# Attention and a highway layer on one core: batch 0 by query tiles, k and v in other layouts, and part of x turned by DMA

## The chip, the cores and the metric

One core of a Trainium2 chip. The metric is device time in microseconds (us), the median of the runs shown. Beside it stands one profiled execution, whose trace all views are taken from. Five engines each work through their own list: PE (TensorE: matrix products), ACT (ScalarE: functions of one operand), DVE (VectorE), POOL (GpSimd) and SP (which only issues DMAs). ACT and POOL issue DMAs too.

## What is computed

Eight batches, twelve heads, 448 positions, 64 dimensions per head. Cosine attention, and then a highway layer on rows of 768 (shortened):

```python
q_n = q / (norm(q) + 1e-6);  k_n = k / (norm(k) + 1e-6)
scores = q_n @ k_n.T / tau
attn = softmax(scores)
x = (attn @ v).transpose(0, 2, 1, 3).reshape(B * S, H * D)     # 3584 x 768
H = relu(x @ w_h);  T = sigmoid(x @ w_t + b_t)
out = T * H + (1 - T) * x
```

## The kernel before

**Layout.** The 448 queries of a head are split as l * 7 + j (64 values of l, 7 of j). q of a batch lies with the even heads on 64 partitions and the odd ones on the other 64, one l to a partition, so that a row of one head is 7 x 64 contiguous numbers (448 numbers, 1,792 bytes). Heads are worked on in six pairs (head p and p + 6), and the pairs in three groups g of two. x of a batch is [128, 7, 384]: FFN tile i of 0 to 2 is the 128 queries of two values of j, with its two halves of the heads in x[:, 2i : 2i + 2]; tile 3, the "tail", is the 64 queries of j = 6, with the two halves of the heads on the two halves of the partitions.

**Per batch,** in the names that the program gives to its operations:

- loads: q in fp32 on SP's queue (`ldq`, L297, L299); k and v cast to fp16 on POOL's queue (`ldk` L309, `ldv` L327 and L331) for the first 384 positions, three to a partition; the last 64 positions of k and v in fp32 on SP's queue (`ldkt` L314, `ldvt` L320). Batch 0 takes k in fp32 into the output buffers `os` instead (`ldf` L305). The gate's and the layer's weights come once, cast, on POOL's queue (L335);
- norms: squares on ACT (L368 q, L388 and L391 k, L402 k's tail), sums over 64 numbers on DVE (L376, L397, L404), then the inverse root by two Newton steps in seven short DVE instructions (L416 to L423, `nt`);
- scaling: POOL multiplies q (L434), k (L495) and k's tail (L502), DVE some of the first; PE turns them (`tq` L446: 7 products with the identity, `tk8` L460 and L465: 8), DVE copies them out of PSUM (L451, L471, L473, L475);
- scores of a pair: three groups `qk` of two products side by side (L531: 64 rows, 128 columns of weights, 448 moving columns) and one `qkt` for the tail (L542); ACT takes the exp of each 128 x 448 (L537, L544), seven per pair;
- values: for each pair three groups `av` (one product L556 and six L561, weights are 128 queries of the exps) and one `avt` for the last 64 queries (L569, 8 products); column 65 of v is 1, so the sum of the exps comes along; DVE takes its reciprocal and writes x (L576, L577, `rc` and `ev`);
- FFN, for each of the four tiles: PE turns x (`xt6` L600, six products with the identity, three in the tail), DVE copies to xT (L602, `cpx`); the gate's and the layer's products (`ff`, halves of three products each: L616, tail L613); DVE adds the bias (L625, `za`), ACT takes tanh (L632), DVE the rest (L634, L628, L637), POOL adds x into `os` (L642, for the last two tiles DVE), SP stores (L649 tail, L652).

**What sets the order.** Nothing is scheduled on the chip. A list ORDER (L18 to L95) gives the order of all 1,915 operations, written out as numbers; SLOTS (L97 to L130) gives each buffer. Every engine works its own part of that list from front to back and waits by semaphores for its operands. `PORT` names operations of DVE and POOL between which the order adds a dependence (L133, L723 to L734). Rings of buffers are small: three E (exps of a pair), three x, three xT, four os, eight PSUM banks B.

Where the text below counts operations, they are counted in ORDER, each number resolved to the operation that the program makes under it.

Of the kernel before, what the change touches and what calls it, by code (L numbers as in the profile page):

```python
# [8 lines left out]
FP32 = mybir.dt.float32  # L9
# [84 lines left out]
""".split()  # L94
)  # L95

SLOTS = {  # L97
    "qr": "01010101",
    "kr": "0120120",
    "kt": "01010101",  # L100
    "kb": "01010101",
    "kp": "012345012345012345012345012345021435021435120534",
    "vr": "01010101",
    "vt": "01011010",
    "vp": "01010101",
    "sq": "0120120102102102102102012012022102102102102021020",
# [95 lines left out]
def kernel(  # L202
# [26 lines left out]
    NN = 84  # L229
# [540 lines left out]
```

## Time and profile before

| | |
|---|---|
| median of 3 runs | 270.19 us (269.24 to 270.47) |
| profiled execution | 270.06 us, of it 268.3 us span |
| PE, DVE, ACT, POOL busy | 251.6, 233.4, 214.5, 169.8 us |
| DMA | 51,092 packets, 38.64 MB; queue of SP 25,888 packets, of POOL 24,896 |
| exps L537 and L544 | 288 and 48 instructions, means 577 and 597 ns (they overlap by some 0.1 us) |
| turns of x L600, copies L602 | 168 and 32 instructions |
| landing of wt, wh, the two weights | 20.3 and 24.3 us after issue |

Busy time counts an engine's instructions from start to end; products of PE overlap, so their mean duration (326 ns for 384 columns) is longer than their distance. Idle time of an engine that others don't wait for costs nothing.

### The profile page before, as it was taken

To read this page: it belongs to the slowest core of one execution; us is meant where nothing else is said; L and a number is where in the kernel's file an instruction comes from. 1 tells how busy PE (TensorE), PEld (TensorE's weight loads), DVE (VectorE), ACT (ScalarE), POOL (GpSimd) and SP (SyncE) were. 2 spreads that over 40 slices of the span, in tenths; PEclk is the share of its full clock that TensorE was granted. 3 is DMA by queue.
4 is the path that set the end of the run, shared out by engine and by line. 5 is a ranking of instruction groups with operands and counts; after the bars stand their busy time and mean duration, and the time that the engine had idled before them with its cause. 6 is when DMAs were issued, how large, how long until landed. Compare 5 with 4: busy or idle time off the path is not lost.

```text
span 268.3 us, 7687 instructions
## 1 busy us (share of the span) xinstructions
PE 251.6 (94%) x3042; PEld 158.8 (59%) x3042; DVE 233.4 (87%) x523; ACT 214.5 (80%) x421; POOL 169.8 (63%) x212
## 2 busy tenths in 40 slices
PE   8375999999999999999999999999999999999990
PEld 2122566656756576657656685666666675667660
DVE  2987988799999999999989899999998788657993
ACT  3389899999589997999899996999979757883120
POOL 6467878306975679668957397659555686320650
PEclk9755799999999999999999999999999999999998
DMA  7999999999307990496995972990513101052146
GB/s 173 298 290 181 208 270 261 213 255 126 44 18 221 234 182 14 146 257 159 151 142 185 164 107 67 330 135 4 147 23 100 29 15 49 0 147 65 29 135 190
DMA packets 51092, 38.64 MB, mean 144 GB/s; under 512 B 37488, under 2 KB 47856, under 8 KB 51056
## 3 DMA queue, kind: packets, MB, share of 16 engines
q1 hardware_dynamic: 25888, 26.75, 36.2%
q0 software_dynamic: 24896, 11.21, 33.1%
q8 instruction: 24, 0.39, 0.5%
q10 hardware_dynamic: 272, 0.20, 0.2%
q14 instruction: 12, 0.10, 0.1%
HBM read 38.34 MB, written 11.01 MB: 184 GB/s over the span
## 4 chain that ended last, share of the span: by engine, by line
PE 81%; DMA 6%; DVE 4%; ACT 4%; SPq 1%; issue 1%; POOL 1%; ACTq 0%; DVEq 0%
PE B L616 33%; PE B L531 12%; PE B L561 10%; PE B L613 5%; DMA os<-in_k_dram 4%; PE B L556 4%; PE B L600 4%; PE B L446 3%; PE B L542 3%; PE B L569 3%; PE B L460 3%; ACT E L537 3%; DMA out_dram<-os 1%; PE B L465 1%; DVE hm L628 1%
## 5 line engine op out<-in xcount | busy, mean ns | idle before, releaser
L537 ACT ACTIVATE E<-B 128x448 f16<-128x448 f32 x288 | 137.4, 577 | 15.6 <-PE B L531 12.6
L642 POOL TENSOR_TENSOR os<-x,hm 128x384 f32<-128x384 f16 x53 | 47.5, 911 | 50.2 <-DVE hm L637 39.6
L616 PEld LDWEIGHTS <-xT 128*128 128x128 f16 x576 | 51.2, 98 | 34.8 <-issue 7.5
L434 POOL TENSOR_TENSOR qn<-qr,y 128x448 f16<-128x448 f32 x47 | 43.4, 934 | 24.6 <-issue 8.1
L616 PE MATMUL B<-wh,xT 128*128 128x384 f16 x288 | 57.6, 326 | 0.0
L616 PE MATMUL B<-wt,xT 128*128 128x384 f16 x288 | 56.7, 326 | 0.0
L531 PE MATMUL B<-qT,kT 64*128 64x448 f16 x288 | 43.5, 367 | 2.8 <-DVE kT L473 1.5
L561 PE MATMUL B<-vp,E 128*128 128x65 f16 x864 | 44.5, 195 | 0.0
L561 PEld LDWEIGHTS <-E 128*128 128x128 f16 x864 | 39.1, 99 | 2.9
L632 ACT ACTIVATE tt<-z 128x768 f16<-128x768 f32 (+1 forms) x32 | 25.3, 793 | 18.5 <-DVE z L625 14.8
L495 POOL TENSOR_TENSOR kp<-kr,y 128x384 f16<-128x384 f16 x42 | 34.3, 827 | 8.2 <-DVE tt L634 2.6
L628 DVE SCALAR_TENSOR_TENSOR hm<-B,x 128x384 f16<-128x384 f32 x56 | 30.5, 549 | 3.0 <-PE B L616 1.7
L556 PE MATMUL B<-vp,Et 128*128 128x130 f16 x144 | 32.3, 224 | 0.0
L625 DVE TENSOR_TENSOR z<-B,bias 128x384 f32<-128x384 f32 x48 | 25.9, 551 | 6.5 <-PE B L616 5.5
L544 ACT ACTIVATE Et<-B 128x448 f16<-128x448 f32 x48 | 27.9, 597 | 3.1 <-PE B L542 2.8
L577 DVE SCALAR_TENSOR_TENSOR x<-B,rd 128x448 f16<-128x448 f32 x48 | 29.2, 617 | 0.6
L376 DVE TENSOR_REDUCE n<-sq 128x14 f32<-128x896 f32 (+1 forms) x25 | 25.8, 1040 | 1.2 <-ACT sq L368 1.2
L397 DVE TENSOR_REDUCE n<-sq 128x18 f32<-128x1152 f32 (+2 forms) x17 | 21.5, 1269 | 4.2 <-ACT sq L388 3.8
L368 ACT ACTIVATE sq<-qr 128x896 f32<-128x896 f32 (+1 forms) x24 | 23.1, 978 | 1.1 <-DMA qr<-in_q_dram 1.1
L531 PEld LDWEIGHTS <-kT 64*128 64x128 f16 x288 | 10.3, 94 | 20.1 <-issue 12.3
L556 PEld LDWEIGHTS <-Et 128*128 128x128 f16 x144 | 14.1, 98 | 7.9 <-issue 4.7
L542 PE MATMUL B<-qT,kT 128*128 128x448 f16 x48 | 17.4, 371 | 1.1 <-DVE kT L475 1.1
(59 smaller groups left out, 363.3 us busy)
## 6 DMA issues: line engine op xcount, KB each, us to landing
qr<-in_q_dram SPq DMA_DIRECT2D x7, 1344.0 KB, 7.6
out_dram<-os SPq DMA_DIRECT2D x48, 192.0 KB, 3.3
kr<-in_k_dram POOLq DMA_DIRECT2D x7, 576.0 KB, 12.2
vr<-in_v_dram POOLq DMA_DIRECT2D x7, 576.0 KB, 10.3
kt<-in_k_dram SPq DMA_DIRECT2D x16, 96.0 KB, 6.4
vt<-in_v_dram SPq DMA_DIRECT2D x16, 96.0 KB, 7.5
out_dram<-os SPq DMA_DIRECT2D x16, 96.0 KB, 2.9
qr<-in_q_dram SPq DMA_DIRECT2D x3, 448.0 KB, 6.9
```

What stands on the lines that cost most here:

```text
L434: ENG[eng].tensor_mul(R("qn", 3 * b + g)[:, :, t, :], R("qr", b)[:, g + 3 * t, :].rearrange("l (j d) -> l j d", d=D), R("y", b)[:, c : c + ...
L495: ENG[eng].tensor_mul(R("kp", 6 * b + p).rearrange("l c t d -> l t c d"), a, kcol(b, p))
L531: nc.tensor.matmul(R("B", ("S", n, c, t))[:, 0:S], lhsT=R("kT", i)[ln, s, 128 * c : 128 * c + 128], rhs=R("qT", i)[ln, s, :], start=True, ...
L537: nc.scalar.activation(R("E", n)[:, at : at + 7, :].rearrange("l j x -> l (j x)"), R("B", ("S", n, c, t))[:, 0:S], AF.Exp)
L544: op("ACT", f"expt {n}", lambda: nc.scalar.activation(R("Et", n).rearrange("l j x -> l (j x)"), R("B", ("St", n))[:, 0:S], AF.Exp), r=[("B ...
L556: nc.tensor.matmul(U[:, 2 * c : 2 * c + 2, :], lhsT=Et[:, 2 * c : 2 * c + 2, :].rearrange("l j x -> l (j x)"), rhs=vp[:, 6:8, 0:65], start ...
L561: nc.tensor.matmul(U[:, 2 * c + t, :], lhsT=E[:, at : at + 2, :].rearrange("l j x -> l (j x)"), rhs=vp[:, 3 * t + m, 0:65], start=False, s ...
L577: op("DVE", f"ev {n}", lambda: nc.vector.scalar_tensor_tensor(out=R("x", b)[:, :, D * p : D * p + D], in0=U_()[:, :, 0:D], scalar=0.0, in1 ...
L616: nc.tensor.matmul(P[:, 0:MH], lhsT=xT[:, cc, :], rhs=w_[:, cc, MH * mh : MH * mh + MH], start=(cc == 0), stop=(cc == CC - 1))
L625: op("DVE", f"za {g} {mh}", lambda at=at, sl=sl: nc.vector.tensor_add(R("z", g)[:, sl], R("B", at)[:, 0:MH], biast[:, :] if tail else bias ...
L628: op("DVE", f"hm {g} {mh}", lambda at=at, sl=sl, mh=mh: nc.vector.scalar_tensor_tensor(out=R("hm", g)[:, sl], in0=R("B", at)[:, 0:MH], sca ...
L642: op(eng, f"out {g} {mh}", lambda sl=sl, mh=mh: ENG[eng].tensor_add(R("os", g)[:, sl], xpart(mh), R("hm", g)[:, sl]), r=[("gg", g), ("x", ...
```

## The change

1. **k by 7 positions like q.** `ldk` loads rows of 448 numbers; squares, sums, scaling and turning of k are those of q, without a separate tail. The scaled k lies in [128, 8, 2, 64] with one zeroed piece at either end, and eight turns per group put the middle six positions into three full blocks and the outer ones into the tail's block.
2. **v in four loads on POOL's queue** per batch (two halves of the heads, two of the partitions, 3 or 4 positions each), tails among them; `vt` copies the tail from there.
3. **Batch 0.** Its k comes in fp32 in three parts, the first on ACT's queue, into E buffers. Its inverse roots are exp(-0.5 ln(n + 1e-14)) on ACT (`lnexp`), for which ACT loads table 6 at the start and table 0 behind the third; tanh waits for that. Its attention runs by query tiles: `attend0(g, i)` for tile i of 128 queries (the fourth has 64) and group g, with exps of 512 and 384 columns, and x has a token of its own for each tile, so that FFN tile i reads only its own queries. The turned q and k of its first group lie in an x buffer.
4. **x of batches 1 to 6** is turned into xT by a transposing DMA on SP's queue (`xd`), without PE and DVE; batches 0 and 7 keep `xt` and `cpx`.
5. Rings: xT 5 (was 3), qT and kT 4 (3), no kt, vt, kb; v's zeroes and ones are set by DVE, not POOL. The loads of q of batches 1 on get a dependence on the ACT instruction ahead of them in the order.
6. ORDER and SLOTS are new throughout (1,875 operations).

In the new order `ldf 0` (ACT) and `ldq 0 0` (SP) come first, POOL starts with `ldk 1`, then v of batch 0 and the gate's weights. The first FFN product belongs to tile 0 of batch 0 and stands behind 25 exps of batch 0 in ACT's list; before, it stood behind 52 exps. All counts of exps by width in the new list: 21 of 512 and 21 of 384 for batch 0, 42 of 448 for each later batch, as before.

The core of the diff:

```diff
-    WARM = 18
+    WARM, NF = 18, 0
+    XDMA = range(1, B - 1)
...
+    LG = ((0, 0), (0, 28), (0, 56))
...
-        xT=(3, [128, CC, 128], FP16), z=(2, [128, DM], FP32), tt=(2, [128, DM], FP16), hm=(3, [128, DM], FP16),
+        xT=(5, [128, CC, 128], FP16), z=(2, [128, DM], FP32), tt=(2, [128, DM], FP16), hm=(3, [128, DM], FP16),
...
+    def ld_kf(g, eng):
+        op(eng, f"ldf {g}", lambda: ENG[eng].dma_start(kf(g), q_src(k, 0)[:, :, g::3, :]), w=[("E", ("f", g))])
...
+    def ld_v(b):
+        for t, jj, j0, n in ((0, 0, 0, 4), (0, 1, 4, 3), (1, 0, 0, 3), (1, 1, 3, 4)):
+            def fn(t=t, jj=jj, j0=j0, n=n):
+                c = 64 if (t, jj) == (0, 1) else 0
+                nc.gpsimd.dma_start(R("vr", b)[64 * jj : 64 * jj + 64, 6 * t : 6 * t + 6, c : c + 64 * n].rearrange("l h (c d) -> l h c d", c=n),
+                                    v_src(b)[:, 6 * t : 6 * t + 6, j0 : j0 + n, :])
+            op("POOL", f"ldv{n} {b} {t} {jj}", fn, w=[("vr", b, t, jj)])
...
+    def lnexp(b, lo, hi, parts):
+        i = (b, lo)
+        op("ACT", f"ln{hi - lo} {b} {lo}", lambda: nc.scalar.activation(
+            R("tu", i)[:, 0, lo:hi], R("n2", b)[:, lo:hi], AF.Ln, bias=eps[:, 0:1]),
...
+        op("ACT", f"ie{hi - lo} {b} {lo}", lambda: nc.scalar.activation(
+            R("y", b)[:, lo:hi], R("tu", i)[:, 0, lo:hi], AF.Exp, scale=-0.5),
...
+    def attend0(g, i):
...
+                        for t in range(2):
+                            ln, at = slice(64 * t, 64 * t + 64), unit(s)[0][t][c] - o - 512 * t
+                            nc.tensor.matmul(R("B", (A, B_)[t])[:, at : at + w], lhsT=k_()[ln, s, 128 * c : 128 * c + 128],
+                                             rhs=q_()[ln, s, 128 * i : 128 * i + w], start=True, stop=True)
...
+            for t, X, m in ((0, A, 512), (1, B_, 384)):
+                op("ACT", f"ex{m} {n}", lambda X=X, m=m, t=t, o=o: nc.scalar.activation(
+                    flat()[:, o + 512 * t : o + 512 * t + m], R("B", X)[:, 0:m], AF.Exp),
...
+        def turn_dma():
+            X = R("x", b)
+            nc.sync.dma_start(R("xT", g)[:, 0:nb, :], X[:, 6, :] if tail else X[:, 2 * i : 2 * i + 2, :].rearrange("l j m -> l (j m)"),
+                              transpose=True)
+        if b in XDMA:
+            op("SP", f"xd{nb} {g}", turn_dma, r=[xk], w=[("xT", g)])
+        else:
+            op("PE", f"xt{nb} {g}", turn_x, r=[xk, ("id",)], w=[("B", ("Tx", g))], mode="F")
...
+    op("ACT", "table2", lambda: table(0), r=[("lg", i) for i in LG], w=[("t0",)])
...
         if b == 0:
...
+            for i in range(4):
+                for g in range(NG):
+                    attend0(g, i)
```

More of the change, by code (lines that the diff above doesn't have):

```diff
@@ L144, in __init__ @@
         kind = name.split()[0].rstrip("0123456789")
-        self.port = eng in ("DVE", "POOL") and (kind in PORT or kind == "sqq")
+        self.held = eng == "SP" and kind == "ldq" and name.split()[1] != "0"
+        self.port = eng in ("DVE", "POOL") and (kind in PORT or kind == "sq")
 class Plan:
@@ L220 @@
     NC, NJ = 3, 7
-    WARM = 18
+    WARM, NF = 18, 0
+    XDMA = range(1, B - 1)
+    GROUPS = ((0, 1), (1, 2), (2, 3)), ((0, 1), (1, 3)), ((0, 3),)
+    LG = ((0, 0), (0, 28), (0, 56))
+    SCALE = {("q", 0, 0): ("DVE", "POOL"), ("k", 0, 0): ("DVE", "POOL")}
     tau = float(tau)
@@ L247 @@
     biast = sb.tile([128, MH], FP32, name="biast")
[L248 removed]
+    eps = sb.tile([128, 1], FP32, name="eps")
     wz = sb.tile([128, 640], FP16, name="wz")
@@ L258, in R16, with turned, tn @@
         return R("B", i).bitcast(FP16)
+    def turned(nm, i):
+        if i:
+            return R(nm + "T", i)
+        X = R("x", "f").rearrange("l j m -> l (j m)")
+        return (X[:, 0:896] if nm == "q" else X[:, 896:1920]).rearrange("l (s x) -> l s x", s=2)
+    def tn(nm, i):
+        return (nm + "T", i) if i else ("x", "f", nm)
     ENG = dict(SP=nc.sync, ACT=nc.scalar, POOL=nc.gpsimd, DVE=nc.vector, PE=nc.tensor)
@@ L267, in zero, with table @@
         return fn
-    op("ACT", "table", lambda: nc.scalar.activation(tab[:1, :], nc.const_aps.tensor(0.0, [1, 1]), AF.Exp), w=[("tab",)])
+    def table(n):
+        return nc.scalar.add_instruction(mybir.InstLoadActFuncSet(
+            name=nc.get_next_instruction_name(), engine=nc.scalar.engine, act_func_set_id=n))
+    op("ACT", "table", lambda: table(6), w=[("t6",)])
     op("POOL", "ident", lambda: make_identity(nc, ident), w=[("id",)])
     for i, t in enumerate(TILES["vp"]):
-        op("POOL", f"zvp {i}", zero("POOL", [(t[:, :, 0:6, D : D + 1], 1.0), (t[:, :, 6:8, 0 : D + 1], 0.0),
+        op("DVE", f"zvp {i}", zero("DVE", [(t[:, :, 0:6, D : D + 1], 1.0), (t[:, :, 6:8, 0 : D + 1], 0.0),
                                     (t[0:64, :, 6, D : D + 1], 1.0), (t[64:128, :, 7, D : D + 1], 1.0)]), w=[("zvp",)])
-    for i, t in enumerate(TILES["kb"]):
-        op("DVE", f"zkb {i}", zero("DVE", [(t[0:64, :, 1, :], 0.0), (t[64:128, :, 0, :], 0.0)]), w=[("zkb",)])
-    op("DVE", "zw", zero("DVE", [(wz[:, :], 0.0)]), w=[("wz",)])
+    for i, t in enumerate(TILES["kn"]):
+        op("DVE", f"zkn {i}", zero("DVE", [(t[:, 0, 1, :], 0.0), (t[:, 7, 0, :], 0.0)]), w=[("zkn",)])
+    op("DVE", "zw", zero("DVE", [(wz[:, :], 0.0), (eps[:, :], 1e-14)]), w=[("wz",), ("eps",)])
     for i in range(WARM):
@@ L280, with q_src, v_src, ld_qk @@
                                                          start=True, stop=True), r=[("wz",)], w=[("B", ("W", i)), ("wm",)], mode="F")
-    def q_src(b):
-        return q[b].rearrange("(u s) (l j) d -> s l u (j d)", s=2, j=NJ)
-    def m_src(t, b):
-        return t[b, :, 0 : NC * 128, :].rearrange("h (l c) d -> l h (c d)", c=NC)
-    def t_src(t, b, ab):
-        return t[b, 6 * ab : 6 * ab + 6, NC * 128 : S, :].rearrange("h l d -> l h d")
-    def ld_q(b, gs=range(3), eng="SP"):
+    for i in range(NF):
+        op("PE", f"wf {i}", lambda i=i: nc.tensor.matmul(R("B", ("F", i))[:, :], lhsT=wz[:, 0:128], rhs=wz[:, 128:640],
+                                                         start=True, stop=True), r=[("wz",)], w=[("B", ("F", i))], mode="F")
+    def q_src(t, b):
+        return t[b].rearrange("(u s) (l j) d -> s l u (j d)", s=2, j=NJ)
+    def v_src(b):
+        return v[b].rearrange("h (l j) d -> l h j d", j=NJ)
+    def ld_qk(nm, b, gs=range(3)):
+        t, eng = (q, "SP") if nm == "q" else (k, "POOL")
         def fn():
-            d, a = R("qr", b), q_src(b)
+            d, a = R(nm + "r", b), q_src(t, b)
             if len(gs) == 3:
@@ L344, in ld_b, with col @@
         op("SP", "ldb", fn, w=[("b",)])
-    QC = (0, 38, 52)
-    KCS = ((14, 26, 32, 66, 72, 78), 20), ((14, 20, 26, 66, 72, 78), 32)
-    def kcol(b, p):
-        return R("y", b)[:, KCS[b > 0][0][p] : KCS[b > 0][0][p] + 6].rearrange("l (t c) -> l t c", t=2).unsqueeze(3).to_broadcast([128, 2, NC, D])
-    def norm_q(b, g, split):
-        i = ("q", b, g)
-        for t in range(2) if split else (None,):
-            ts = slice(0, 2) if t is None else slice(t, t + 1)
-            n = 2 if t is None else 1
-            eng = "DVE" if t == 1 else "ACT"
-            def src(ts=ts):
-                return R("qr", b)[:, g::3, :][:, ts]
-            def dst(ts=ts):
-                return R("sq", i)[:, 0:896].rearrange("l (t x) -> l t x", t=2)[:, ts]
-            def fn(eng=eng, src=src, dst=dst):
+    def col(nm, g):
+        return 28 * g + 14 * (nm == "k")
@@ new lines, with source, token, norm @@
+    SQV = ()
+    SPLIT = {("q", 0, 0): ("ACT", "DVE"), ("k", 0, 0): ("ACT", "ACT")}
+    def source(nm, b, g):
+        return kf(g) if nm == "k" and b == 0 else R(nm + "r", b)[:, g::3, :]
+    def token(nm, b, g):
+        return ("E", ("f", g)) if nm == "k" and b == 0 else (nm + "r", b, g)
+    def norm(nm, b, g):
+        i = (nm, b, g)
+        sc = tau if nm == "q" else 1.0
+        engs = SPLIT.get(i, (("DVE" if i in SQV else "ACT"),))
+        n = 3 - len(engs)
+        for t, eng in enumerate(engs):
+            ts = slice(t, t + n)
+            def fn(eng=eng, ts=ts):
+                src = source(nm, b, g)[:, ts]
+                dst = R("sq", i).rearrange("l (t x) -> l t x", t=2)[:, ts]
@@ L437, in fn, with turn @@
                     R("y", b)[:, c : c + 7].unsqueeze(2).to_broadcast([128, NJ, D]))
-            op(eng, f"qn {b} {g} {t}", fn, r=[("qr", b, g), ("y", b, "q", g)], w=[("qn", 3 * b + g, t)])
-    def turn_q(b, g, parts):
+            op(eng, f"{nm}n {b} {g} {t}", fn, r=[token(nm, b, g), ("y", b, nm, g)], w=[(nm + "n", i, t)])
+    def turn(nm, b, g):
         i = 3 * b + g
+        at = ("T" + nm, i)
+        nj = NJ if nm == "q" else 8
         def fn():
-            T = R16(("Tq", i))[:, 0:896].rearrange("p (s j l) -> p j s l", s=2, j=NJ)
-            for j in range(NJ):
-                nc.tensor.transpose(T[:, j], R("qn", i)[:, j].rearrange("l t d -> l (t d)"), ident[:, :])
-        op("PE", f"tq {b} {g}", fn, r=[("qn", i, 0), ("qn", i, 1), ("id",)], w=[("B", ("Tq", i))], mode="F")
-        for s in range(2) if parts == 2 else (None,):
-            def cp(s=s):
-                a = slice(0, 896) if s is None else slice(448 * s, 448 * s + 448)
-                nc.vector.tensor_copy(R("qT", i).rearrange("p s x -> p (s x)")[:, a], R16(("Tq", i))[:, a])
-            op("DVE", f"cpq{parts} {b} {g} {s}", cp, r=[("B", ("Tq", i))], w=[("qT", i, s)] if s is not None else [("qT", i, 0), ("qT", i, 1)])
@@ L498, in scale_kb @@
-    def scale_kb(b, eng):
-        for ab in range(2):
-            def fn(ab=ab):
-                ln, c = slice(64 * ab, 64 * ab + 64), KCS[b > 0][1]
-                ENG[eng].tensor_mul(R("kb", b)[ln, :, ab, :], R("kt", b)[ln, :, :],
-                                    R("y", b)[ln, c : c + 6].unsqueeze(2).to_broadcast([64, NP, D]))
-            op(eng, f"kb {b} {ab}", fn, r=[("kt", b), ("zkb",), ("y", b, "t")], w=[("kb", b)])
+            T = R16(at)[:, 0 : 128 * nj].rearrange("p (s j l) -> p j s l", s=2, j=nj)
@@ new lines, in fn @@
+            for j in range(nj):
+                to = j if nm == "q" else 2 * ((j - 1) % 3) + (j - 1) // 3 if 0 < j < 7 else 6 + (j == 7)
+                nc.tensor.transpose(T[:, to], R(nm + "n", i)[:, j].rearrange("l t d -> l (t d)"), ident[:, :])
+        op("PE", f"t{nm} {b} {g}", fn, r=[(nm + "n", i, 0), (nm + "n", i, 1), ("id",)] + ([("zkn",)] if nm == "k" else [])
+           + ([("wm",)] if i == 0 and nm == "k" else []), w=[("B", at)], mode="F")
+        op("DVE", f"cp{nm} {b} {g}", lambda: nc.vector.tensor_copy(
+            turned(nm, i), R16(at)[:, 0 : 128 * nj].rearrange("p (s x) -> p s x", s=2)), r=[("B", at)], w=[tn(nm, i)])
@@ L583, in ffn, with turned_of @@
+    def turned_of(g):
+        return lambda: turned("q", g), lambda: turned("k", g)
     def ffn(b, i):
         g = 4 * b + i
+        xk = ("x", b) if b else ("x", b, i)
         tail = i == 3
@@ L700 @@
-        scale_kb(b, "POOL")
-        if b == 0:
-            copy_v(b, 0, 3)
-            copy_v(b, 3, 6)
-        else:
-            copy_v(b, 0, 6)
-        cast_vt(b, "POOL")
-        for g in range(NG):
-            first = b == 0 and g == 0
-            scale_q(b, g, ("DVE", "POOL") if first else ("POOL", "POOL"))
-            for s in range(2):
-                scale_k(b, 2 * g + s, "DVE" if first else "POOL")
-            turn_q(b, g, 2 if first else 1)
-            turn_k(b, g)
-        for p in range(NP):
-            scores(b, p)
-            attend(b, p)
+        if b < 2:
+            for g in range(NG):
+                ld_qk("q", b, [g])
+                if b == 0:
+                    ld_kf(g, "SP" if g else "ACT")
+            if b:
+                ld_qk("k", b)
+            ld_v(b)
+            if b == 0:
+                ld_w(moe_w_t, wt, "wt")
+                ld_w(moe_w_h, wh, "wh")
+                ld_b()
+        else:
+            ld_qk("q", b)
+            ld_qk("k", b)
+            ld_v(b)
@@ new lines @@
+        for g in range(NG):
+            for nm in "qk":
+                norm(nm, b, g)
+        for g0, g1 in GROUPS[min(b, 2)]:
+            (lnexp if (b, 28 * g0) in LG else newton)(b, 28 * g0, 28 * g1, [(nm, g) for g in range(g0, g1) for nm in "qk"])
+        for p0 in (0, 3) if b == 0 else (0,):
+            copy_v(b, p0, p0 + (3 if b == 0 else 6))
+        copy_vt(b, "POOL")
+        for g in range(NG):
+            for nm in "qk":
+                scale(nm, b, g, SCALE.get((nm, b, g), ("POOL", "POOL")))
+                turn(nm, b, g)
@@ L717, with behind @@
+        if b == 0:
+            for i in range(4):
+                for g in range(NG):
+                    attend0(g, i)
+        else:
+            for p in range(NP):
+                scores(b, p)
+                attend(b, p)
         for i in range(4):
             ffn(b, i)
+    def behind(a, b):
+        tc.add_manual_dep(a, b.name, mybir.DependencyInfo(mybir.DependencyClass.Sync, mybir.DependencyReason.SCHED_ONLY),
+                          reason="order")
     with nc.allow_low_precision(reason="fp16 operands of the products and gates as given"):
@@ L721 @@
         with tc.manual_schedule():
-            before = None
+            before = act = None
             for o in pl.ordered(ORDER, SLOTS):
@@ L725 @@
                 o.fn()
-                if o.port:
-                    made = [i for i in nc.cur_bb.bb.instructions[made:] if i.engine == ENG[o.eng].engine]
-                    if o.eng == "DVE":
-                        before = made[-1]
-                    elif before is not None:
-                        tc.add_manual_dep(made[0], before.name, mybir.DependencyInfo(
-                            mybir.DependencyClass.Sync, mybir.DependencyReason.SCHED_ONLY), reason="port")
-                        before = None
+                made = [i for i in nc.cur_bb.bb.instructions[made:] if i.engine == ENG[o.eng].engine]
+                if o.eng == "ACT":
+                    act = made[-1]
+                elif o.held:
+                    behind(made[0], act)
+                elif o.port and o.eng == "DVE":
+                    before = made[-1]
+                elif o.port and before is not None:
+                    behind(made[0], before)
+                    before = None
 _INS = ['q', 'k', 'v', 'tau', 'moe_w_h', 'moe_w_t', 'moe_b_t']
```

317 lines of the change are left out of this document (126 added, 191 removed), and 145 rows, old and new, of the table ORDER.

## The prediction

> **What bounds the kernel now.** I read the page first: the busy line, then the slices.
>
> ```profile
> PE 251.6 (94%) x3042; PEld 158.8 (59%) x3042; DVE 233.4 (87%) x523; ACT 214.5 (80%) x421; POOL 169.8 (63%) x212
> ...
> PE   8375999999999999999999999999999999999990
> ...
> ACT  3389899999589997999899996999979757883120
> ...
> PEclk9755799999999999999999999999999999999998
> DMA  7999999999307990496995972990513101052146
> ```
>
> TensorE (PE) has the most work, and after slice 5 it is never idle. Its gaps, and its halved clock, are in the first 30 us, where the DMA engines are full. ACT is the next dense engine until slice 27. The table of windows says how dense (columns: window, its length, busy us and instructions of PE, weight loads, DVE, ACT, POOL, then clock, DMA share, GB/s):
>
> ```profile
> 7.00:14.00 7.00, 2.24 (x15) 1.23 (x13) 6.43 (x24) 1.98 (x4) 3.76 (x5) 0.73 1.18 304
> 14.00:21.00 7.00, 5.28 (x22) 1.47 (x22) 6.16 (x18) 6.35 (x13) 4.04 (x5) 0.50 1.25 272
> 21.00:28.00 7.00, 4.75 (x22) 2.03 (x22) 5.51 (x16) 6.95 (x14) 6.39 (x9) 0.50 1.44 181
> ...
> 35.00:42.00 7.00, 6.95 (x106) 4.14 (x103) 6.77 (x19) 7.00 (x17) 4.10 (x6) 1.00 1.11 268
> ...
> 70.00:100.00 30.00, 30.00 (x388) 19.39 (x386) 29.45 (x66) 26.40 (x54) 21.80 (x27) 1.00 0.70 146
> ```
>
> So there are three stages: a start in which ACT, fed by DMA, sets the pace; a long stage in which PE is full (30.00 of 30), with DVE 29.45 and ACT 26.40 close behind; and 6.3 us after PE's last product (the window from 262.0 on holds two of its instructions). The chain that ended last, in order of time, gives the prices of PE's work (start, us, line, count):
>
> ```profile
> 45.86 2.06 PE B L616 x12
> ...
> 68.97 1.95 PE B L613 x24
> 70.92 0.50 PE B L446 x7
> 71.42 1.00 PE B L600 x18
> 72.87 1.46 PE B L616 x9
> ```
>
> Three products of a gate take 0.487 us (1.46 / 9 x 3), seven turns of q 0.50, six turns of x 0.33 (0.39 elsewhere in this view). The FFN of batch 0 begins at 45.86, that of batch 1 at 72.87, and PE works from there to 262.0 without a pause: 189.1 us.
>
> **x turned by DMA.** Six batches lose 3 x 6 + 3 = 21 turns on PE and four copies on DVE each.
>
> ```profile
> L600 PE MATMUL B<-ident,x 128*128 128x128 f16 x168 | 13.4, 219 | 0.0
> L602 DVE COPY xT<-B 128x768 f16<-128x768 f16 x24 | 12.8, 549 | 0.7 <-PE B L600 0.7
> L602 DVE COPY xT<-B 128x384 f16<-128x384 f16 x8 | 2.8, 349 | 0.2 <-PE B L600 0.2
> ```
>
> PE: 126 turns at 57 ns (0.34 us for six elsewhere in the chain) are 7.2 us, at the row's 13.4 / 168 = 80 ns 10.0 us; I use 0.36 us for six, 7.6. DVE: 18 x 0.549 + 6 x 0.349 = 12.0 us, hidden behind PE either way (DVE 87%). In their place 24 DMAs on SP's queue, which the trace of before does not have. The nearest row moves the same 196,608 bytes on the same queue, the stores:
>
> ```profile
> out_dram<-os SPq DMA_DIRECT2D x48, 192.0 KB, 3.3
> ```
>
> Over the span that is the median; the line view gives 2.6 to 7.8, and the issues of 60 to 110 us, where the loads of later batches run beside them, a median of 6.2, those of 110 to 160 us 5.0, of 160 to 210 us 2.7. I take 5.0 for issue to landing: five of the six turned batches run beside loads, but the new loads have fewer packets. PE needs 4 x 0.36 us less, but the first tile of a batch now waits for that landing, where a turn and its copy took 0.39 + 0.55. An xd that waits for x holds back what follows on SP, stores and q loads: SP already stands 69.3 us behind POOL's sums at L652, and four os buffers cover it; I price that at nothing, and at one more store's 3.3 us if the cover fails.
>
> By the Trainium skill (DMA: Bandwidth & Descriptors, section Latency and other measured facts) a transposing DMA moves 261 GB/s where the middle dimension is not contiguous; as an estimate from that page the data take 0.75 us of the landing. No run here shows it yet; by it the landing would be near the stores' low end, and the sum near 260.
>
> **Loads, norms, scaling.** k as q needs 768 packets of 1,792 bytes a batch in place of 1,536 of 768 and 768 of 256; v 1,536 in place of 1,536 and 768. In the start, where the DMA share is over 1, that is some 2,300 packets less for batch 0, but group 0's k grows from 192 to 448 KB, and the k of batch 1 stands first on POOL's queue, beside it. The first k landed after 4.8 us here, a 448 KB part of q after 6.9; so I put the first square at 6.5 us, against 5.57. Per batch, POOL loses two kb (2 x 0.852), its six scalings grow from 0.827 to 0.934 (+0.6), and v's issues go from 1.07 to four of 0.806 (+2.2): +1.1 us at 63% busy, hidden. Squares and sums keep their element counts (2,688 a batch). SP loses 32 issues of kt and vt.
>
> **Batch 0.** Its scores have the same 42 exps, half of them 512 wide and half 384; PE pays some 0.7 us more for short moving operands (weights are loaded for 128 columns in place of 448), DVE 12 evictions in place of 6 (+1.8), both in the stage that ACT leads. Newton's chain (8.30 to 10.10 us, seven steps) becomes an Ln and an Exp, 0.25 us each by the smallest ACT row (0.19) and a wait. The second table load costs ACT 1.28 us (the row at 1.26 us): bounds 1.28 and, if the engine must empty before it, one exp more, 1.86.
>
> The Trainium skill (ScalarE: Activation LUTs, section What ACT_TABLE_LOAD costs) adds a drain of about 1.38 us to each switch; before's only load stands ahead of all work and can't show it. By it the sum below is 1.4 us larger.
>
> **Where ACT now decides.** The order list, counted per engine, says what ACT must have done before the last exp of batch 1. Before: 72 exps at 0.435 (the chain has 0.87 for two) and 12 at 0.45, 9 squares of q at 0.93, five k squares of 1,152 at 1.15, six small ACT ops 3.1, two tanh at 0.8: 55.5 us. The trace ends that exp at 66.8: ACT had 11.3 us of lead and idleness (5.57 to the first data, then 1.71, 1.11 and 2.82, plus crumbs). After: 21 pairs of exps (0.87 a pair, by width), 42 exps 18.4, 16 squares at 0.93, three halves 1.6, six Ln and Exp 1.5, the table 1.28, two tanh 1.6: 57.5 us. The start is 0.9 later, but batch 1's squares stand ready to fill the wait for the first scores: I take 10.9 of idleness (9.0 to 13 as bounds). So that exp ends at 68.4; the last product, its reciprocal and eviction take 2.0 (0.25 + 0.2 + 0.62 and waits), the DMA 5.0: batch 1's FFN begins at **75.4**, though PE would be there at about 71.7 (batch 0's first FFN product, which no longer waits for all queries, at about 34 in place of 45.86, plus 37.7 us of PE's list between). The earlier start of batch 0's FFN is worth little: it uses up early what PE had to do while ACT worked on batch 1.
>
> From there PE's list holds, before, 168 + 28 FFN halves, 108 pairs of scores, 36 tails, 17 + 17 turns of q and k, 108 + 36 groups of value products, 18 + 7 turns of x. At the chain's prices (FFN half 0.487, pair 0.235, tail 0.19, q 0.50, k 0.60, value groups 0.25 and 0.125, x 0.36 and 0.18) that is 185.6 us, and the trace took 189.1 (factor 1.019). After: the same but 103 pairs, 33 tails, 16 + 16 turns, and only 3 + 1 turns of x: 176.3, with the factor 179.6.
>
> **The sum.** 75.4 + 179.6 = 255.0. Batches 2 and 3 by the same rule: ACT's list to their last exps is 86.2 and 113.9, so 104.1 and 131.8, 0.6 and 0.2 later than PE: +0.8. In batch 4 the order leaves 4.4 us of PE's work between x and its first product, against 5.0: +0.6. The end is as before (same ops, same os waits, which DVE's work hides): 6.3. Span 262.7. Before, the profiled execution took 270.06 for a span of 268.3, 1.8 more: **264.5 us**. The median shown is 270.19, 0.1 above the profiled one; that is no correction.
>
> **Rivals.** *PE alone decides* (0.25): ACT loses less at the start (9.0) and transposes land in 2.7, so batch 1 begins at 71.6: 71.6 + 179.6 + 6.3 + 1.8 = 259.3. For it: light DMA after 160 us, fewer packets. Against: ACT at 7.00 of 7 in 35 to 42. *Slower: the transposes land late* (0.20). PE's order is fixed, so each of six first tiles holds it. At the stores' 7.8 that is 2.8 x 6 = 16.8 more, 281.3; it decides from 5.0 + 5.6 / 6 = 5.9 us, where the gain is gone, and the 6.2 of 60 to 110 us is above that. Against: the last batches run without loads. *A late start* (0.05): q, k and batch 1's k share the DMA engines, the first scores come 5 us later, 269.5. *The forecast* has 0.50. That the DMAs do not turn x is excluded by the code; that PE stays as full as before is the first rival.
>
> **Numbers.** The range takes in the first rival and half of the second: 257 to 272. About 0.5% is what a measurement of this kernel can tell from no change: faster 0.75 (forecast and first rival), within 0.09 (late start, transposes near 5.9), slower 0.16 (the rest of the second).
>
> **What would show it.** L600 with 42 turns; first FFN products of batches 0 and 1 at 34 and 75 us; PE idle some 4 us for xT around 71 to 76 and full later; landings of xT near 5 us; ACT at 95% or more from 15 to 130 us. Wrong if PE waits for xT in every batch, if ACT idles over 13 us in the start, or if PE is never idle after 34.

## The result, and the profile after

The changed kernel takes **261.54 us** (median of 4, 261.1 to 262.53), the kernel before beside it 270.33: a ratio of 0.9682, 95% interval 0.9636 to 0.9727. Measured again it took 261.8 (median of 5), ratio 0.9682 (0.9657 to 0.9706). The forecast was 264.5. Medians and ratios are of executions within 1.5% of the kernel's fastest; three executions of two kernels lie outside (309.06, 309.13 and 310.92). The profiled execution took 262.53 for a span of 260.7, so what lies around the span is 1.8 us, as before.

Busy line and slices of the page of the changed kernel:

```profile
PE 244.0 (94%) x3042; PEld 155.7 (60%) x3042; DVE 221.1 (85%) x486; ACT 215.8 (83%) x425; POOL 169.4 (65%) x210
...
PE   7378999999999999999999999999999999999990
...
ACT  3699999999999999999798999989988768692130
...
PEclk9955999999999999999999999999999999999998
```

PE has as many instructions as before (x3042): 126 turns of x went, and the rest of the change put as many smaller products in. ACT now reads 9 from the third slice on, and the clock is back at full speed after four slices. The table of windows (columns as before):

```profile
14.00:21.00 7.00, 5.32 (x55) 3.60 (x55) 5.95 (x8) 6.78 (x13) 5.36 (x7) 0.50 1.31 227
21.00:28.00 7.00, 6.41 (x97) 4.86 (x94) 5.74 (x13) 6.63 (x13) 6.08 (x9) 0.64 1.11 289
...
35.00:42.00 7.00, 7.00 (x130) 5.08 (x129) 6.21 (x20) 7.00 (x16) 4.87 (x7) 1.00 1.22 265
```

From 21 to 28 us PE is now busy 6.41 of 7 in place of 4.75. The turns that are left, and the line that sums up the landings of the transposing DMAs (line 637):

```profile
L633 PE MATMUL B<-ident,x 128*128 128x128 f16 x42 | 3.3, 220 | 0.0
```

```profile
DMA to landing us min/median/max: 2.3/2.8/8.4
```

**Where the time went.** An exact price list was needed first. The starts of PE's products show what the prediction's prices mixed: an FFN half takes 0.487 us when another product of the full array follows (146 cases after 75 us) and 0.583 when a pair of scores follows (15 cases); a value group 0.248 or 0.34 the same way, a pair of scores 0.19 to 0.2 among its like and 0.285 before anything else. So every change of the tile form (full array, halves of rows, halves of columns) costs 0.095 us, and there are 112 of them from batch 1's first FFN product on. The prices without it: pair 0.194, tail 0.189, q turned 0.389, k 0.445, six turns of x 0.335, three 0.167. Summed over the order list, against the trace (us):

| | before | after |
| --- | --- | --- |
| first FFN product of batch 0 | 45.8 | 31.7 |
| first FFN product of batch 1 | 72.7 | 72.0 |
| PE's list up to there, at full clock (batch 0's small products priced roughly) | 51.1 | 54.0 |
| so waits and half clock up to there | 21.6 | 18.0 |
| PE's list from there to its end | 187.3 | 178.6 |
| the trace's time for it | 189.2 | 181.7 |
| so waits there | 1.9 | 3.1 |
| PE's end to the end of the span | 6.4 | 7.0 |

PE's list is 8.7 shorter from batch 1 on: 15 turns of six and 6 of three (6.0), 5 pairs and 3 tails of scores (1.5), one turn of q and of k (0.8) and three changes of form (0.3) that now stand in the start, and rounding. In both kernels PE waits for nearly nothing after 72 us. In sum: 7.0 off for all 126 turns, 1.2 on for batch 0 by tiles, 3.6 off in the start's waits and half clock, 1.2 and 0.6 on in later waits and the end: 7.6 of the span. Half clock has 1.6 of the 3.6: it is granted from 10.2 to 30.6 us before and from 12.4 to 26.1 after, and half of PE's busy time in it is 7.0 and 5.4 us.

### The profile page after: what moved, and what is told of

The parts are those of the page before. It is cut to its first block, busy times and chain, and to the rows that moved or that the text cites. A ratio compares the mean times of both kernels' runs of the same rounds, so it can differ in the third digit from the quotient of the medians.

```text
span 260.7 us, 7685 instructions
## 1 busy us (share of the span) xinstructions
PE 244.0 (94%) x3042; PEld 155.7 (60%) x3042; DVE 221.1 (85%) x486; ACT 215.8 (83%) x425; POOL 169.4 (65%) x210
## 4 chain that ended last, share of the span: by engine, by line
PE 76%; DMA 8%; ACT 6%; DVE 5%; POOL 2%; issue 2%; DVEq 0%; ACTq 0%; POOLq 0%
PE B L657 32%; PE B L473 10%; PE B L503 8%; PE B L442 6%; PE B L654 6%; DMA kr<-in_k_dram 5%; DMA xT<-x 3%; PE B L498 3%; ACT E L479 3%; PE B L484 3%; PE B L511 3%; PE B L577 1%; PE B L550 1%; DVE n L385 1%; ACT sq L377 1%
## 5 line engine op out<-in xcount | busy, mean ns | idle before, releaser
L479 ACT ACTIVATE E<-B 128x448 f16<-128x448 f32 x252 | 122.8, 599 | 11.5 <-PE B L473 8.7
L385 DVE TENSOR_REDUCE n<-sq 128x14 f32<-128x896 f32 (+1 forms) x50 | 50.9, 1039 | 1.4 <-ACT sq L377 1.3
L425 POOL TENSOR_TENSOR kn<-kr,y 128x448 f16<-128x448 f16 x42 | 38.8, 934 | 6.2 <-DVE hm L678 2.7
L503 PE MATMUL B<-vp,E 128*128 128x65 f16 x756 | 38.3, 193 | 0.0
L673 ACT ACTIVATE tt<-z 128x768 f16<-128x768 f32 (+1 forms) x32 | 26.1, 819 | 14.7 <-DVE z L666 14.7
L669 DVE SCALAR_TENSOR_TENSOR hm<-B,x 128x384 f16<-128x384 f32 x56 | 30.6, 550 | 6.4 <-PE B L657 5.2
L503 PEld LDWEIGHTS <-E 128*128 128x128 f16 x756 | 33.6, 97 | 3.6 <-issue 0.6
L473 PE MATMUL B<-qT,kT 64*128 64x448 f16 x252 | 35.2, 354 | 0.0
L377 ACT ACTIVATE sq<-qr 128x896 f32<-128x896 f32 (+1 forms) x24 | 22.9, 991 | 4.2 <-DMA qr<-in_q_dram 4.2
L335 POOL DMA_DIRECT2D vr<-in_v_dram x32 | 21.9, 690 | 1.0 <-DVE vp L451 0.8
L377 ACT ACTIVATE sq<-kr 128x896 f32<-128x896 f16 x21 | 21.8, 1063 | 0.6 <-DMA kr<-in_k_dram 0.6
L563 ACT ACTIVATE E<-B 128x384 f16<-128x384 f32 (+1 forms) x42 | 20.5, 592 | 0.4 <-PE B L550 0.3
L442 PE MATMUL B<-ident,kn 128*128 128x128 f16 x192 | 15.7, 227 | 4.8 <-DVE kn L425 2.5
```

The lines of the kernel that those rows point to most:

```text
L377: nc.scalar.activation(dst, src, AF.Square, scale=sc)
L385: nc.vector.reduce_sum(R("n2", b)[:, c : c + 7 * n], a, axis=AX.X)
L425: ENG[eng].tensor_mul(R(nm + "n", i)[:, o : o + NJ, t, :], source(nm, b, g)[:, t].rearrange("l (j d) -> l j d", d=D), R("y", b)[:, c : c + ...
L442: nc.tensor.transpose(T[:, to], R(nm + "n", i)[:, j].rearrange("l t d -> l (t d)"), ident[:, :])
L473: nc.tensor.matmul(R("B", ("S", n, c, t))[:, 0:S], lhsT=R("kT", i)[ln, s, 128 * c : 128 * c + 128], rhs=R("qT", i)[ln, s, :], start=True, ...
L479: nc.scalar.activation(R("E", n)[:, at : at + 7, :].rearrange("l j x -> l (j x)"), R("B", ("S", n, c, t))[:, 0:S], AF.Exp)
```

## The experiments

**Is it the turns? Take them out of the kernel before; put them back into the changed one.** In the kernel before:

```diff
         def turn_x():
+            if g in range(4, 28):
+                return
             for j in range(nb):
...
-        op("DVE", f"cpx{nb} {g}", lambda: nc.vector.tensor_copy(
+        op("DVE", f"cpx{nb} {g}", lambda: None if g in range(4, 28) else nc.vector.tensor_copy(
```

> The kernel before, without the turns of x and their copies for batches 1 to 6 (the FFN of these batches reads x turned of batch 0, so this work is left out; nothing is put in its place). Theory T: 270.2 less 7.6 us of TensorE's list, 262.6 (261.5 to 264), without any edit of the start, and the same to 1 us as the changed kernel. Rival R1 (start): 267 to 270. Rival R2 (ACT holds batch 1's FFN at its old 72.7 whatever TensorE has to do): batch 1's first FFN product stays within 0.5 us of 72.8, and the time falls by 7 us all the same, so the two part on where TensorE waits and not on the time.

Measured: 268.93 us, ratio 0.9946 (0.9918 to 0.9974), so 1.6 us less and not 7.6. PE's list from batch 1 on is 181.2 and the trace took 188.7: 7.5 us of waits in place of 1.9. The chain's shares in the kernel before, then in this run:

```profile
PE 81%; DMA 6%; DVE 4%; ACT 4%; SPq 1%; issue 1%; POOL 1%; ACTq 0%; DVEq 0%
```

```profile
PE 50%; DVE 15%; POOL 13%; ACT 11%; issue 6%; DMA 3%; POOLq 0%; SPq 0%; DVEq 0%; ACTq 0%
```

With the same order list and 6.1 us less for PE to do, the chain runs through DVE, POOL and ACT by turns. No one of them is the new bound. A reading that fits, though no run isolates it: the order had each of them just in time for a PE that had the turns to do. The time lies in the range of rival R1 (the gain is the start), 267 to 270; by the table above the start's waits and half clock are 3.6 of the 7.6, so the start is a part of the gain and not all of it.

In the changed kernel (each turn and copy put some 1 us of PE's work behind the DMA's old place, 24 buffer slots following):

```diff
-    XDMA = range(1, B - 1)
+    XDMA = ()
```

> The changed kernel, with x of all batches turned on TensorE and copied by VectorE again, at places some 1 us of TensorE work behind the place of the DMA in the order; all else of the change stays. Theory T (TensorE's list sets the time from 32 us on, and the 126 turns taken off it are nearly the whole gain): the list grows by 21 turns of six at 0.36 us, 7.6, so 261.5 + 7.6 = 269.1 us (268 to 271 with some waits for copies), that is about as before. Rival R1 (the gain is the start: batch 0 by tiles, lighter loads, ACT): the time stays at 261.5 to 264. Rival R2 (the prediction's own step, ACT holds batch 1 and the turns fill idle TensorE time): batch 1's first FFN product moves by less than 1 us and the time by 5 to 6 us, 267.

Measured: 284.46 us, ratio 1.0541 (1.0499 to 1.0583): 22.9 more than the changed kernel, three times theory T's price. PE's list from batch 1 on is 185.6, the trace took 202.7. Waits of PE, then of DVE (us in total, times, longest):

```profile
PE B L658 <- DVE xT L644: 4.3, 7, 0.7
```

```profile
DVE xT L644 <- PE B L634: 12.6, 14, 1.6
```

DVE stands 12.6 us before copies whose turns PE has not yet done, and all that is queued behind the copy waits too. The run misses both rivals too. What the two runs share: in an order this tight, a step was worth what its place was worth (1.6 us taken out, 22.9 put back), not what its work is by the list (6.1 and 7.6).

**Which engine holds the start, and what do the landings cost?** Three edits of the changed kernel, beside that kernel itself.

> The changed kernel once more, as the measure for the runs beside it: 261.5 us (260.5 to 262.5).

Measured: 261.8 us; batch 0's first FFN product at 32.0, batch 1's at 72.28.

```diff
-    op("ACT", "table2", lambda: table(0), r=[("lg", i) for i in LG], w=[("t0",)])
+    op("ACT", "table2", lambda: (table(0), table(6), table(0)), r=[("lg", i) for i in LG], w=[("t0",)])
```

> The changed kernel with three table loads in place of one in the middle of batch 0 (2 x 1.28 us more on ACT at 24 us; the tables loaded twice are read by nothing). Theory T (ACT has slack ahead of batch 1's FFN, TensorE does not): 0 to 1 us more than the changed kernel, and batch 1's first FFN product moves by less than 1 us. Rival R2 (ACT's list decides there, as the prediction had it): the last exp of batch 1 and its first FFN product move by 2.6 us, and the time by 2.6, 264.1. If each load also drains the engine for 1.4 us, ACT loses 5.4 us, and by R2 the time is 267.

Measured: 265.12 us, ratio 0.9801 (0.9774 to 0.9829): 3.3 more. Both first products move by 3.1 (35.08 and 75.36), the last exp of batch 1 too (66.27 to 69.36), and everything behind it by as much. But PE's clock differs as well; its slices in the kernel beside it, then in this run:

```profile
PEclk9955999999999999999999999999999999999996
```

```profile
PEclk9865589999999999999999999999999999999997
```

The kernel beside it has half clock from 13.1 to 26.8 us, this run from 10.7 to 17.5 and from 20.9 to 34.6; half of PE's busy time in it is 5.4 and 8.5 us. So this trace alone does not tell the loads on ACT (2.57) from the clock (3.1), and both half-clock stretches began ahead of the loads at 23.5. Two executions of this run have a mean granted clock of 0.964, within the 0.964 to 0.971 of the kernel beside it, and still took 263.86 and 264.97, 2.1 and 3.2 more. So theory T (0 to 1 us) falls and ACT has no such slack in the start, as the prediction had it; how the 3.1 divide stays open. The distance of the two first products is 40.3 us in both runs, and between them both engines are full (ACT 39.84 of 40 from 32 to 72 us, PE's list some 38): which of them sets the pace there, these runs do not tell. ACT's timeline (start, duration, line) also prices a load:

```profile
21.52 1.96 ACT L563 ACTIVATE E<-B 128x384 f16<-128x384 f32 x4
23.50 3.86 ACT L282 ACT_TABLE_LOAD   x3
27.37 6.95 ACT L563 ACTIVATE E<-B 128x512 f16<-128x512 f32 x15
```

Three loads take 3.86 us, with exps 0.02 before and 0.01 behind them. No longer gap stands here or at the single load; what is lost besides is the 0.1 us by which two exps overlap.

```diff
-            nc.sync.dma_start(R("xT", g)[:, 0:nb, :], ...
+            for _ in range(2):
+                nc.sync.dma_start(R("xT", g)[:, 0:nb, :], ...
```

> The changed kernel with each transposing DMA issued twice, one behind the other on SP's queue, into the same buffer, so that x turned is ready about one more issue (1.24 us) and at most one more landing (2.8 us) later: 4 to 5.6 us in place of 2.8. Theory T (the order leaves 3.6 to 4.4 us of TensorE work between the DMA and the first product on it): 0.3 to 1 us a batch beyond the cover, 2 to 6 us in all, 263.5 to 267.5. By the prediction's slower rival, whose price was one us for each us of landing in six batches: 6 x 2.8 = 16.8 us more, 278; by its midpoint, 6 x 1.24 = 7.4, 269.

Measured: 306.67 us, ratio 1.1332 (1.1278 to 1.1386): 44.9 more, far past every expectation. The waits of SP and of PE say why:

```profile
SPq L638 <- DMA xT<-x: 56.0, 24, 6.8
```

```profile
PE B L658 <- DMA xT<-x: 29.2, 10, 6.7
```

The second DMA writes what the first wrote, so SP waits 2.3 us on average (56.0 / 24) for the first to land, which the expectation had forgotten: each tile holds SP some 3.6 us longer (2.3 + 1.24), and SP comes to the next tile as much later. Counted from its x, a batch's first tile is turned 2.7 to 3.0 us later than in the kernel beside it (6.0 once), the second 5.6 to 10.4; their first products start 0.4 to 4.1 and 0.8 to 7.3 us later. The slower rival had priced one us for each us of landing on six first tiles. Here the second tiles cost more, since SP's queue carries the delay on. PE's clock adds to it:

```profile
PEclk9857999998899999999879998799999997799997
```

Behind batch 1's first product it is halved in four stretches, 23.9 us in all (74.5 to 77.9, 149.5 to 156.4, 187.1 to 193.9, 255.4 to 262.2). Each begins within a wait of PE for x turned or 0.5 us behind it, and half of PE's busy time in them is 7.6 us. So the 44.9 are not the price of longer landings alone, which was not run.

```diff
-            op("SP", f"xd{nb} {g}", turn_dma, r=[xk], w=[("xT", g)])
+            op("SP", f"xd{nb} {g}", lambda: None, r=[xk], w=[("xT", g)])
```

> The changed kernel with no transposing DMA at all (x of batches 1 to 6 is not turned, their FFN reads what batch 0 left in the buffers; SP loses 24 issues, and no product waits for x turned). What is left of the landings goes. Theory T (landings of 2.8 us are covered but for some 1.4 us of waits that the trace puts to them, 0.9 of them in one batch behind a load of q): 0.5 to 1.5 us less than the changed kernel, 260 to 261. Rival (each of six batches waits for its landing beyond what the trace shows): 3 to 6 us less, 256 to 258.

In this run VectorE also sets two of the xT buffers to zero at the start. Measured: 261.62 us, ratio 0.968 (0.9655 to 0.9704), the same as with the DMAs. The landings as they are (2.8) cost nothing that can be measured; with each DMA issued twice the kernel lost 44.9. Batch 1's first FFN product comes at 72.24 with no landing at all, against 72.28: it waits for PE's place in the order, not for x.

**Is it the order?** Four kernels have an order and buffer slots of their own, found by moving operations in the list and summing each engine's prices. Two are the kernel before, as it is and with x by DMA; two are the changed kernel, as it is and with x turned on PE.

> The kernel before, its operations unchanged, with another order of them (and the buffer slots that follow), found by moving operations about in the order list and adding up, per engine, the prices of the trace's rows. Three theories, since taking the turns out of the kernel before gave 1.6 us and putting them back into the changed kernel cost 22.7. T2 (the turns are worth what their work costs, but only in an order made for them): the order alone gives little that is not the change's; by the prices the new order comes to a span of 262, but no more than 3 us of that should be real, 266 to 269. R3 (the change's gain is its new order and not its edits): 261 to 263, all of the gain without an edit. R1 (start): no change, 270.

> The kernel before with one edit of the change, x of batches 1 to 6 turned by DMAs (five xT buffers in place of three), and an order found in the same way; batch 0, k and v as before. T2: 5 to 9 us less than the kernel before in its new order, and within 3 us of the changed kernel in its new order; by the prices a span of 254. R3: within 1 us of the kernel before in its new order. R1: no gain from this edit, all of it missing: 268 to 270.

> The changed kernel, its operations unchanged, in an order found in the same way. By the prices a span of 253 in place of 259 for its own order. T2 and R3 alike: 255 to 261; it is the mate of the other three, so that the four differ by edits and not by whose order is better.

> The changed kernel with x of all batches turned on TensorE (as in the first run of this study), in an order found in the same way. By the prices a span of 258. T2: 4 to 8 us more than the changed kernel in its new order, and far from the 284.5 of the first run, whose rest was the order's fault. R3: the same as the changed kernel in its new order, to 1 us. R1 (start): 4 us or more below the kernel before in its new order, since batch 0, k and v are the change's.

Measured: 298.3, 300.97, 307.81 and 303.44 us (ratios 1.1042, 1.1149, 1.1391, 1.1229, each to 0.006). All four missed by some 30 to 50 us, and no theory can be judged by them; they show only what an order can cost. PE's list hardly changed (179.1 for the third, from batch 1 on), its waits and half clock rose to 32; from 87 us on the clock is halved for 20.4 us. The prices also lacked a rule. The rows of the gate's first half (line 675), in the changed kernel and in the third of these:

```profile
L675 DVE TENSOR_SCALAR tt<-tt 128x768 f16<-128x768 f16 x24 | 8.9, 377 | 0.2 <-ACT tt L673 0.2
```

```profile
L675 DVE TENSOR_SCALAR tt<-tt 128x768 f16<-128x768 f16 x24 | 25.3, 1059 | 2.4 <-ACT tt L673 2.3
```

And one stretch of the third kernel, POOL's timeline and then DVE's:

```profile
171.49 0.70 POOL L335 DMA_DIRECT2D vr<-in_v_dram  x1
172.18 0.52 POOL L461 COPY vp<-vr 64x384 f16<-64x384 f16 x1
172.65 1.83 POOL L425 TENSOR_TENSOR qn<-qr,y 128x448 f16<-128x448 f32 x2
174.44 1.82 POOL L425 TENSOR_TENSOR kn<-kr,y 128x448 f16<-128x448 f16 x2
```

```profile
171.43 5.06 DVE L675 TENSOR_SCALAR tt<-tt 128x768 f16<-128x768 f16 x2
176.41 0.55 DVE L666 TENSOR_TENSOR z<-B,bias 128x384 f32<-128x384 f32 x1
```

Two gate halves of 0.35 us take 5.06, as long as POOL goes on without a gap (0.94 us of scaling from 170.61 stands ahead of these lines). Counted over this run, gate halves that overlap no POOL operation (DMA issues aside) take 0.35 (13 of 24), those that do 1.9 on average, up to 4.79; DVE operations that read PSUM (z, hm, x) keep their 0.55 to 0.62 either way. The Trainium skill (SBUF — State Buffer, section Who interferes with whom) has the rule: VectorE's second port is GpSimd's only one, an exclusive lock, and the order of issue decides who blocks. The trace agrees that VectorE stands while GpSimd works; that it stands while five operations follow each other, from 172.18 to 176.26, only the trace shows. The PORT list of the kernel holds a POOL operation back behind the DVE operation ahead of it in the order, but not the other way about; these four kernels have it too.

**The order with that rule.** Two more, on the kernel before and on it with x by DMA; the start keeps its order.

```diff
+    XDMA = range(1, B - 1)
...
-        xT=(3, [128, CC, 128], FP16), ...
+        xT=(5, [128, CC, 128], FP16), ...
...
+        if b in XDMA:
+            op("SP", f"xd{nb} {g}", turn_dma, r=[("x", b)], w=[("xT", g)])
+        else:
```

> The kernel before, operations unchanged, with a new order from batch 1's FFN on, found as in the four runs before but with one rule more, read from those runs: VectorE's operations from SBUF to SBUF (the halves of the gate, Newton's steps, copies of v) and GpSimd's do not run at the same time. The start keeps its order. T2 (the gain is TensorE work that goes, in an order that keeps TensorE fed): nothing is taken off TensorE, so 268 to 271, as before. R3 (the gain is the order): 262 to 265. If the rule is not what made the four orders slow, 280 or more again.

> The kernel before with x of batches 1 to 6 turned by DMAs as the one edit of the change (five xT buffers), the start's order kept, the rest ordered by the same rule as its mate; batch 0, k and v as before. T2: TensorE's list is 7 us shorter, so 263 to 266, 4 to 7 us less than its mate. R3: as its mate, to 1 us. R1 (the gain is batch 0, k and v): 268 to 271.

Measured: 272.16 us, ratio 1.0082 (1.0055 to 1.0108), and 274.58, ratio 1.0163 (1.013 to 1.0197). With the rule and the old start both are 26 us faster than without. Of that, 9.3 and 7.5 us lie ahead of batch 1's first product, where the old start came back along with the rule; so the share of the rule by itself is not shown. R3, that any new order brings the gain, has no support: the first is no faster than the old order (though another might be). But x by DMA alone is not faster either, against T2. The second's list from batch 1 on is 181.8 and the trace took 190.2. Between the first FFN products of batches 0 to 4 its PE loses 2.7, 3.6, 1.4 and 2.0 us against its list, in each later stage 0.1 to 0.7; 1.7 of the 3.6 is half clock, granted from 74.4 to 77.8 behind a wait for the turned k. Its landings in full:

```profile
DMA to landing us min/median/max: 2.3/3.0/11.6
```

From 130 to 165 us their median is 5.8, in the changed kernel 4.3. The kernel before has more small packets (under 512 bytes 37,488; the changed kernel without its transposes has 8,112); that these make the landings longer is a reading, not shown, since the orders differ too.

## Why the prediction was right, point by point

**Direction and size** were right: 264.5 forecast, 261.5 measured (262.5 the profiled execution). Batch 1's first product came 3.4 us earlier than forecast; the stage behind it and the end took 0.7 us more each.

**Batch 1's first FFN product**: 75.4 forecast, 71.97 measured, and this is the step that failed. Its terms: ACT was busy for 56.5 us up to batch 1's last exp, forecast 57.5; lead and idleness were 9.5 and not 10.9 (first data at 5.84, not 6.5; of the rest the largest are 1.2 for the first norms and 0.9 each for q and k), so the exp ended at 66.0; the landing was 2.8 and not 5.0. That gives 56.5 + 9.5 + 2.0 + 2.8 = 70.8, below the 71.97 measured, and with no landing the product came no earlier. So the path was wrong at its last step: x turned was there 1.0 us ahead of the product, which waited for PE's place in the order, and there the first rival (PE alone, 71.6) held. The forecast's own sign, PE idle some 4 us for xT around 71 to 76, did not come: from 34 to 130 us PE was idle for 1.1 us in all, close to "never idle after 34", which the prediction had named as a sign of being wrong. That ACT limits the start fits the run with three table loads, as far as its clock lets one say; it was 97% busy from 15 to 130 us, forecast 95% or more. That it does so through the scores PE works on is argued; that it does not by x's landing is shown.

**The stage behind**: 179.6 + 0.8 + 0.6 forecast, 181.7 measured. The list was right (by exact prices 8.7 shorter, forecast 9.3); the factor 1.019 was no slowness of PE: about half of it is prices too low (the list of before is 187.3 and not 185.6; they had the changes of tile form only in part), half waits (1.9). Batch 0 by tiles took 1.2 us more of PE, forecast 0.7 for its short products. The two small waits came elsewhere: PE stood 0.5 us, once, for a transpose of batch 1 that landed in 8.4. It was issued 0.5 us behind a 1,344 KB load of q on the same queue, which landed 1.6 us before it:

```profile
75.53 8.40 DMA xT<-x
...
83.98 0.66 PE B L657 x3
```

**The landing**, 5.0 forecast, 2.8 measured: the stores beside loads were the wrong neighbour, those of 160 to 210 us (2.7) the right one. The Trainium skill's rate (DMA: Bandwidth & Descriptors, Latency and other measured facts, 261 GB/s) had led to the low end, and the trace agrees with that end; the rate itself is not measured here. Between 129 and 158 us, beside loads, the median is 4.3.

**The second table load** took its 1.28 us, and no gap but 0.02 and 0.01 us stands around it; the drain of 1.38 that the Trainium skill adds (ScalarE: Activation LUTs, What ACT_TABLE_LOAD costs) is not in this trace.

**The end**, 6.3 forecast, is 7.0 by the same count that gives 6.4 before: a size.

**The slower rival** did not come, because the first product on x turned starts 3.9 to 5.3 us after x is there in each batch (6.6 or more on a batch's second tile), and the landings on first tiles were 2.7 to 2.9. That PE stands when x turned is late was right; the run with each DMA twice shows that its price, by first tiles alone, was too low for a delay that also holds SP's queue.

**What was right by luck**: the sum took 9.3 us off a full PE's list and let the time of that stage fall by as much. In the order of before, taking 6.1 us of turns off the list gave 1.6. The changed kernel's order keeps PE fed with the shorter list (3.1 us of waits from batch 1 on, 1.9 before), and the prediction never asked whether it would.

**What stays open**: how much of the 8.7 us x by DMA would give without the new layout of k and v. The order found for it waits up to batch 4's FFN, and whether a better one exists was not settled; nor what turns on PE would cost in the changed kernel in an order made for them. No run has the new start (batch 0 by tiles, k and v) in the kernel before without the other edits, so its share of the gain is the table's sum and not a measurement.

## What to carry to other kernels

Where the order of every engine is fixed and three of them are over 80% full, sum the bound engine's list from the starts of its instructions and compare it with the trace: the difference is what that engine loses to waits and a lower clock. Work taken off in an unchanged order may come back as waits; here 6.1 us gave 1.6. Ask of a moved step what is queued behind it on its engine: its place can cost three times its work. Two experiments say this quickly, the step left out where it was and the step's delay doubled where it is. Compare the granted clock of the runs first: a lower clock can come with waits, as in the run with each DMA twice.

## What the runs showed of the hardware

A change of the matmul's tile form costs PE 0.095 us: 0.583 against 0.487 for an FFN half, 0.34 against 0.248 for a value group, 0.285 against 0.19 for a pair of scores, all from the starts of products in the changed kernel. The Trainium skill (TensorEngine Tiling (Array Packing), Key Properties) says that a change of mode drains the engine and has no price; with 112 changes in the changed kernel from batch 1 on it is 10.6 us, more than all the turns that the change took away.

A DVE operation from SBUF to SBUF can be kept out by a run of POOL operations for as long as they follow each other: 4.79 us for 0.35 of work. Table loads stand back to back at 1.28 us each. A transposing DMA of 196,608 bytes within SBUF landed in 2.7 to 2.9 us in 14 of 18 cases of the changed kernel, in 4.2 to 4.9 in three and in 8.4 in the one issued right behind a 1,344 KB load on its own queue.

The clock granted to PE was halved for some 3.4 us or a multiple of it: 20.4 us in the start of the kernel before, 13.7 in that of the changed one, and 23.9 us in four stretches (3.4 to 6.9 each) of the run with each DMA twice, each begun within a wait of PE or 0.5 us behind it.
